# Decode attention over 64 heads: K and V loaded from two queues, PV moved in front of the next pair's score matmuls, both output weights loaded last

## The chip, the core and the metric

The kernel runs on one core of a Trainium2 chip. The metric is the device time of one execution in microseconds; shown before the change are three runs, with a median of 674.88 us (674.65 to 674.92). Smaller is better. Names of engines: PE is TensorE, DVE is VectorE, ACT is ScalarE, POOL is GpSimd, SP is SyncE. SP and ACT can both issue DMA transfers, each into a queue of its own.

## What is computed

Two independent attention blocks, A and B, each with one query token, 32 heads, 8192 cached keys and values and a head size of 128, all bf16. The outputs of the two are joined.

```python
B, Sq, D = 1, 1, 512
H, Sk, Dh = 32, 8192, 128
q = (x @ wq).reshape(B, Sq, H, Dh)          # by head
scores = einsum("bhqd,bhkd->bhqk", q, k_cache) * Dh ** -0.5
p = softmax(scores)
o = einsum("bhqk,bhkd->bhqd", p, v_cache)
y = o.reshape(B, Sq, H * Dh) @ wo            # 4096 x 512
```

B has as many key heads as query heads, so both blocks are the same in shape. K and V of one head are 2 MB each; wq and wo of a block are 4 MB each.

## The kernel before, in words

The 64 heads are worked on in 32 pairs (`NP`), 16 of A and then 16 of B. A pair's two heads lie on the two halves of the 128 partitions: each partition holds 128 rows (`T`) of one head, 32 KB. So one `load_k(n)` and one `load_v(n)` are one transfer of 4096 KB each. K has two buffers in SBUF (`kn`), V two (`vn`).

A small recorder (`_Plan`) takes the operations in program order, one list for each engine, with the semaphore waits between them; each engine then runs its own list strictly in order. On PE the lists of pairs 3 to 28 are a loop of two pairs a round (`L0, L1 = 3, 29`); all else is straight code.

For pair n the steps are:

- `plan_mul` (DVE, line 292): K is multiplied in place by the query, in four quarters.
- `plan_red` (PE, line 301): 32 matmuls against an identity, in two halves of 16, sum the products over eighths of the head size into PSUM. The end of the second half, `red_done[n]`, frees the K buffer for `load_k(n + 2)`.
- `plan_sr` (DVE, line 310): the rest of the sum gives the scores. `plan_max`, `plan_gmax` and the first part of `plan_exp` (lines 316, 322, 325, 335, 339) find each head's maximum and hand it to all partitions.
- `plan_exp` (ACT, line 346): exp, with its row sums.
- `plan_sum` (PE and DVE, lines 351 and 354): the total of the row sums and its reciprocal.
- `plan_pv` (PE, line 367): 128 matmuls with a V tile as weights and two columns of probabilities. Its end, `pv_done[n]`, frees the V buffer for `load_v(n + 2)`.
- `plan_o` (DVE, line 377): the result, divided by the sum.

The order is a software pipeline written out by hand. In step n of the main loop PE runs: sum of pair n-1, score matmuls of pair n (both halves), first half of PV of pair n-1, the maximum's transpose of pair n, second half of PV of pair n-1, the maximum's broadcast of pair n.

All large loads are issued by SP, in this order: wq of A, K0, wq of B (into the second V buffer), then in step n K(n+1), waiting for `red_done[n-1]`, and V(n), waiting for `pv_done[n-2]`. Wo of A follows V12, into the buffer `wbuf` that held wq of A. At step 29 PE does the wo matmuls of A (`plan_relayout`, `plan_wo`, `plan_y`, lines 402 to 426); then the first half of wo of B (heads 0 to 15) is loaded into the same buffer, and the rest of it in four groups (8, 4, 2, 2 heads, `WOG`) behind V31. V31 is loaded in two halves. The wo matmuls of B's first half stand at the end of step 31, those of the rest after PV of pair 31. `plan_out` transposes the result and stores it.

ACT's own queue has only the two loads of x, 1 KB each.

Of the kernel before, what the change touches and what calls it, by code (L numbers as in the profile page):

```python
# [11 lines left out]
P = 128  # L12
# [11 lines left out]
class _Plan:  # L24
# [6 lines left out]
    def wait(self, eng, mark):  # L31
        if mark is None:
            return
        ctr, val = mark
        if val <= 0 or self.waited.get((eng, ctr.name), 0) >= val:
            return
        self.waited[(eng, ctr.name)] = val
        self.prog[eng].append((None, ctr, val))

    def op(self, eng, fn, ctr=None, needs=(), inc=1):  # L40

        for m in needs:
            self.wait(eng, m)
        self.prog[eng].append((fn, ctr, inc))
        if ctr is None:
            return None
        ctr.n += inc
        return ctr, ctr.n
# [46 lines left out]
def bass_concat_heads__mha_block_cached__gqa_block_cached__decode_kernel(  # L95
# [18 lines left out]
    NA = 2  # L114
    H, Sk, Dh = ks[0].shape[1:]
    D = xs[0].shape[2]
    NOUT = wos[0].shape[1]
# [19 lines left out]
    with ExitStack() as st:  # L137
# [8 lines left out]
        wbuf = sb("wbuf", [P, C * H * Dh], BF16)  # L146
        wq_buf = [wbuf[:], vn[:, 1].rearrange("p t d -> p (t d)")]
        wq_sb = [b.rearrange("p (c n) -> p c n", c=C) for b in wq_buf]
        wo_sb = wbuf[:].rearrange("p (j n) -> p j n", n=NOUT)
        qbc = sb("qbc", [P, NP, Dh], BF16)  # L150
        pt = sb("pt", [P, 2, T, 2], BF16)
        s_sb = sb("s_sb", [P, 2, T], F32)
# [34 lines left out]
        def ctr(name):  # L187
            return _Ctr(nc, st, name)

        s_x = ctr("s_x")  # L190
        s_w = [ctr("s_w%d" % a) for a in range(NA)]
        s_wo = [ctr("s_wo%d" % i) for i in range(5)]
        s_v2 = ctr("s_v2")
        s_k = [ctr("s_k%d" % i) for i in range(NK)]
        s_v = [ctr("s_v%d" % i) for i in range(NV)]
        s_out = ctr("s_out")
# [3 lines left out]
        def dma(eng, dst, src, c, needs=()):  # L200
            return op(eng, lambda e: e.dma_start(dst, src), c, needs, inc=16)  # L201
# [27 lines left out]
            k_in[n] = dma("SP", kn[:, n % NK].rearrange("p t d -> p (t d)"), src, s_k[n % NK],  # L229
                          [red_done.get(n - NK)])  # L230

        def load_v(n, parts=1):
            a, i = divmod(n, PA)
            src = vs[a][0, 2 * i:2 * i + 2].rearrange("h (p t) d -> (h p) (t d)", p=HP)
            dst = vn[:, n % NV].rearrange("p t d -> p (t d)")
            w = T * Dh // parts
            v_in[n] = [dma("SP", dst[:, i * w:(i + 1) * w], src[:, i * w:(i + 1) * w],
                           s_v2 if i else s_v[n % NV],
                           [q_done[1] if n == 1 else pv_done.get(n - NV)])
                       for i in range(parts)]  # L240

        def load_wq(a):
            wq_in[a] = dma("SP", wq_buf[a], wqs[a].rearrange("(p c) n -> p (c n)", p=P), s_w[a])
# [1 line left out]
        def load_wo(a, g):  # L245
            h0, n = WOG[a][g]
            src = wos[a][h0 * Dh:(h0 + n) * Dh, :].rearrange("(p j) n -> p (j n)", p=P)
            wo_in[a, g] = dma("SP", wo_sb[:, h0:h0 + n, :].rearrange("p j n -> p (j n)"), src, s_wo[g],
                              [q_done[0] if a == 0 else wo_done[0]])


        for a in range(NA):
# [37 lines left out]
        def plan_mul(n, c):  # L290
            k = kn[:, n % NK, c * CT:(c + 1) * CT, :]
            mul_done[n, c] = op("DVE", lambda e: e.tensor_tensor(  # L292
                k, k, qbc[:, n:n + 1, :].broadcast_to([P, CT, Dh]), ALU.mult),
                c_mul, [k_in[n], qbc_ready[n]])
# [14 lines left out]
        def plan_sr(n, h):  # L309
            sr_done[n, h] = op("DVE", lambda e: e.tensor_reduce(  # L310
                s_sb[:, n % 2, h * HT:(h + 1) * HT],
                rps[:, h, :].rearrange("p (t d) -> p t d", d=DW), AX.X, ALU.add),
                c_sr, [red_done[n], p_done.get(n - 2)])
# [36 lines left out]
        def plan_sum(n):  # L350
            m = op("PE", lambda e: e.matmul(misc[:, 0:2], ones_f[:], rsum[:, n % 2, :],  # L351
                                            start=True, stop=True), c_pe,
                   [p_done[n], misc_free[0]])
            r_done[n] = misc_free[0] = op("DVE", lambda e: e.reciprocal(  # L354
                rinv[:, n, :], misc[:, 0:2]), c_dve, [m])

        def plan_pv(n, t0, t1):
            parts = v_in[n]
            for i in range(t0 * len(parts) // T, (t1 * len(parts) - 1) // T + 1):
                wait("PE", parts[i])  # L360
            wait("PE", p_done[n])
            wait("PE", o_done.get(n - 2))

            def mm(e):
                r = None
                for t in range(t0, t1):
                    r = e.matmul(acc[:, n % 2, 0:2], vn[:, n % NV, t, :], pt[:, n % 2, t, :],  # L367
                                 start=(t == 0), stop=(t == T - 1))
                return r
            if t1 == T:  # L370
                pv_done[n] = op("PE", mm, c_pv)
            else:
                op("PE", mm)

        def plan_o(n):
            a, i = divmod(n, PA)
            o_done[n] = op("DVE", lambda e: e.tensor_tensor(  # L377
                oD[:, a, 2 * i:2 * i + 2], acc[:, n % 2, 0:2], rinv[:, n, :], ALU.mult),
                c_dve, [pv_done[n], r_done[n]])
# [16 lines left out]
        def plan_relayout(a, g):  # L396
            h0, n = WOG[a][g]
            z = z_n[0] % 2
            z_n[0] += 1
            s = P // n  # L400
            zv = zb[:, z, :].rearrange("p (h s) -> p h s", s=s)
            m = op("DVE", lambda e: e.tensor_tensor(  # L402
                zv, oD[:, a, h0:h0 + n].unsqueeze(2).broadcast_to([P, n, s]),
                mask[n][:, None, :].broadcast_to([P, n, s]), ALU.mult),
                c_dve, [sel_ready[n], o_done[a * PA + (h0 + n) // 2 - 1], z_free.get(z)])
            z_free[z] = op("PE", lambda e: e.matmul(misc[:, 0:n], zb[:, z, :], jsel[n][:],  # L406
                                                    start=True, stop=True), c_pe, [m, misc_free[0]])
            o2_ready[a, g] = misc_free[0] = op("DVE", lambda e: e.tensor_copy(
                o2[:, a, h0:h0 + n], misc[:, 0:n]), c_dve, [z_free[z]])

        def plan_wo(a, g):

            h0, n = WOG[a][g]

            def mm(e):
                r = None
                for j in range(h0, h0 + n):
                    for i in range(NQ):
                        r = e.matmul(qyp[:, i:i + 1], wo_sb[:, j, i * P:(i + 1) * P],  # L419
                                     o2[:, a, j:j + 1], start=(j == 0 and i == 0),  # L420
                                     stop=(j == H - 1 and i == NQ - 1), skip_group_check=True)
                return r
            wo_done[a] = op("PE", mm, c_pe, [o2_ready[a, g], wo_in[a, g], qy_free[0]])

        def plan_y(a):
            qy_free[0] = op("DVE", lambda e: e.tensor_copy(yT[:, a, :], qyp[:, 0:NQ]), c_dve,  # L426
                            [wo_done[a]])
# [7 lines left out]
            wait("SP", done)  # L435


        L0, L1 = 3, 29
        marks = {}

        load_wq(0)
# [5 lines left out]
        for n in range(NP + 1):  # L447
            marks[n] = len(pl.prog["PE"])
            last = n == NP
            if n == L1:  # L450
                plan_relayout(0, 0)
                plan_wo(0, 0)
                plan_y(0)
            if n + 1 < NP:
                load_k(n + 1)
            if n == 1:
                for j in range(4):
                    plan_q(1, j)
            if not last:
                load_v(n, 2 if n == NP - 1 else 1)  # L460
            if n == 12:
                load_wo(0, 0)
            if n == L1:
                load_wo(1, 0)
            if n == NP - 1:
                for g in range(1, len(WOG[1])):
                    load_wo(1, g)
            if not last:
                plan_mul(n, 0)
                plan_mul(n, 1)  # L470
            if n > 0:
                plan_sum(n - 1)
            if not last:
                plan_red(n, 0)
                plan_mul(n, 2)
                plan_mul(n, 3)
                plan_sr(n, 0)
                plan_red(n, 1)
            if n > 0:
                plan_pv(n - 1, 0, HT)  # L480
            if not last:
                plan_sr(n, 1)
                plan_max(n)
                plan_gmax(n)
            if n > 0:
                plan_pv(n - 1, HT, T)
            if not last:
                plan_exp(n)
            if n > 0:
                plan_o(n - 1)  # L490
            for g, (h0, k) in enumerate(WOG[1]):
                if n == max(L1 + 1, PA + (h0 + k) // 2):
                    plan_relayout(1, g)
            if n == NP - 1:
                plan_wo(1, 0)
        for g in range(1, len(WOG[1])):
            plan_wo(1, g)
        plan_y(1)
        plan_out()
# [40 lines left out]
```

## Time and profile before

| | |
|---|---|
| median of three runs | 674.88 us |
| the profiled execution, its own time | 674.97 us |
| its span, first to last instruction | 673.2 us |
| bytes read | 285.21 MB, 424 GB/s over the span |
| PE, DVE, ACT busy | 70%, 53%, 7% |
| mean granted clock of PE | 0.738 |
| score matmuls (line 301), 1024 | 293.2 us busy |
| multiplies (line 292), 128 | 286.8 us busy |
| PV (line 367), 4096 matmuls | 113.0 us busy |
| an issue of a large transfer on SP | 0.33 us |
| K, issue to landing, median | 25.5 us in A, 25.3 in B |
| V, issue to landing, median | 31.6 us in A, 31.4 in B |

The profile is of one execution. Its times are counted from the start of the span; "idle before" is how long an engine stood before an instruction, and what ended that. The chain of waits is followed back from the last instruction, at each step to what released it. In tables by stretch, each engine has its busy time and number of instructions, and then come the granted clock of PE as a share of full speed, the mean busy share of the 16 DMA engines, and the GB/s that they moved. DMA queue q1 is SP's and q10 is ACT's.

### The profile page before, as it was taken

The page shows a single profiled execution, that of the slowest core. Times are in us where ns is not written, and L with a number is a line of the kernel's source. Part 1 is how long each engine was busy: PE and PEld are TensorE (multiplying, and loading weights), DVE is VectorE, ACT ScalarE, POOL GpSimd, SP SyncE. Part 2 cuts the span into 40 slices and gives each one's busy share as a digit, 9 for nine tenths or more (in the row PEclk, how much of TensorE's full clock was granted, in tenths as well). Part 3 has the DMA queues.
Part 4 walks back from the last instruction along what each step waited for, and adds up shares of the span by engine and source line. Part 5 has one row for each costly group of instructions (what it writes and reads, how often), then busy time and mean ns, then how long its engine had stood idle before and what let it go on. Part 6 is the DMA issues. An engine that isn't in the chain of part 4 may idle for free.

```text
span 673.2 us, 12408 instructions
## 1 busy us (share of the span) xinstructions
PE 468.9 (70%) x5712; PEld 275.8 (41%) x5712; DVE 359.4 (53%) x345; ACT 43.9 (7%) x171; POOL 2.1 (0%) x13
## 2 busy tenths in 40 slices
PE   2575887566778776665667787676677776778857
PEld 1233444244444343442344444344444433455526
DVE  1554556565555665615655556566555565645451
ACT  1120000000000000000000000000000000000000
POOL 1000000000000000000000000000000000000000
PEclk9787877667788766776677887666778765677866
DMA  9999999999999999999999999999999999999994
GB/s 374 436 435 431 429 423 432 427 434 436 433 430 432 430 428 432 434 434 430 431 432 428 432 432 436 428 432 434 428 430 432 436 427 434 432 429 429 427 424 202
DMA packets 10550, 285.48 MB, mean 424 GB/s; under 512 B 1186, under 2 KB 1188, under 8 KB 1572
## 3 DMA queue, kind: packets, MB, share of 16 engines
q1 hardware_dynamic: 10528, 285.22, 98.7%
q8 instruction: 13, 0.21, 0.1%
q14 instruction: 5, 0.04, 0.0%
q10 hardware_dynamic: 4, 0.00, 0.0%
HBM read 285.21 MB, written 0.00 MB: 424 GB/s over the span
## 4 chain that ended last, share of the span: by engine, by line
DMA 61%; PE 26%; DVE 8%; issue 5%; SPq 0%
DMA kn<-in_A_k_cache_dram 31%; DMA kn<-in_B_k_cache_dram 30%; PE rps L301 23%; DVE kn L292 7%; PE acc L367 2%; PE qyp L419 1%; PE mtp L322 0%; PE bmp L430 0%; DVE zb L402 0%; PE bmp L335 0%; PE misc L406 0%; PE misc L351 0%; SPq L201 0%; DVE oD L377 0%; DVE yT L426 0%
## 5 line engine op out<-in xcount | busy, mean ns | idle before, releaser
L301 PE MATMUL rps<-kn,ident 128*128 128x512 bf16 x1024 | 293.2, 457 | 144.0 <-DVE kn L292 144.0
L292 DVE TENSOR_TENSOR kn<-kn,qbc 128x4096 bf16<-128x4096 bf16 x128 | 286.8, 2283 | 90.9 <-DMA kn<-in_A_k_cache_dram 63.3
L301 PEld LDWEIGHTS rps<-kn,ident 128*128 128x128 bf16 x1024 | 114.2, 114 | 310.4 <-DVE kn L292 140.5
L367 PEld LDWEIGHTS acc<-pt,vn 128*128 128x128 bf16 x4096 | 110.6, 97 | 14.8 <-issue 7.5
L310 DVE TENSOR_REDUCE s_sb<-rps 128x64 f32<-128x512 f32 x64 | 44.3, 691 | 132.2 <-PE rps L301 132.2
L367 PE MATMUL acc<-pt,vn 128*128 128x2 bf16 x4096 | 113.0, 164 | 0.5 <-issue 0.5
L339 ACT ACTIVATE negb<-bmp 128x1 f32<-128x1 f32 x32 | 5.5, 171 | 594.4 <-PE bmp L335 594.4
L351 PE MATMUL misc<-rsum,ones_f 128*128 128x2 f32 x64 | 18.2, 354 | 36.7 <-ACT pt L346 36.4
L351 PEld LDWEIGHTS misc<-rsum,ones_f 128*128 128x128 f32 x64 | 15.5, 301 | 39.6 <-ACT pt L346 38.8
L377 DVE TENSOR_TENSOR oD<-acc,rinv 128x2 bf16<-128x2 f32 x32 | 5.1, 159 | 48.3 <-PE acc L367 48.3
L346 ACT ACTIVATE pt<-s_sb,negb 64x128 bf16<-64x128 f32 x64 | 27.9, 435 | 1.8
L335 PE MATMUL bmp<-gm,hrow 1*128 1x1 f32 x128 | 23.6, 285 | 0.5 <-DVE gm L325 0.5
L325 DVE TENSOR_REDUCE gm<-mtp 1x2 f32<-1x128 f32 x32 | 8.9, 279 | 27.8 <-PE mtp L322 27.8
L335 PEld LDWEIGHTS bmp<-gm,hrow 1*128 1x128 f32 x128 | 21.0, 230 | 1.3 <-issue 0.7
L322 PE MATMUL mtp<-ident_f,m 128*1 128x128 f32 x64 | 12.1, 271 | 1.1 <-DVE m L316 1.1
L346 ACT ACTIVATION_READ_ACCUMULATOR pt<-s_sb,negb 64x1 f32 x64 | 11.7, 182 | 0.0
L274 PE MATMUL qyp<-wbuf,xb 128*64 128x512 bf16 x32 | 5.6, 484 | 6.2 <-DMA wbuf<-in_A_wq_dram 4.1
L316 DVE TENSOR_REDUCE m<-s_sb 128x1 f32<-128x128 f32 x32 | 9.2, 286 | 1.1
L419 PE MATMUL qyp<-o,wbuf 128*128 128x1 bf16 x256 | 7.3, 165 | 1.1 <-issue 0.9
L419 PEld LDWEIGHTS qyp<-o,wbuf 128*128 128x128 bf16 x256 | 7.0, 102 | 1.3 <-issue 0.9
L274 PE MATMUL qyp<-vn,xb 128*64 128x512 bf16 x32 | 5.5, 477 | 2.3 <-ACT qbc L282 2.3
L354 DVE RECIPROCAL rinv<-misc 128x2 f32<-128x2 f32 x32 | 5.3, 164 | 2.9 <-PE misc L351 2.9
(34 smaller groups left out, 27.1 us busy)
## 6 DMA issues: line engine op xcount, KB each, us to landing
kn<-in_A_k_cache_dram SPq DMA_DIRECT2D x16, 4096.0 KB, 25.5
vn<-in_A_v_cache_dram SPq DMA_DIRECT2D x16, 4096.0 KB, 31.6
kn<-in_B_k_cache_dram SPq DMA_DIRECT2D x16, 4096.0 KB, 25.3
vn<-in_B_v_cache_dram SPq DMA_DIRECT2D x15, 4096.0 KB, 31.4
wbuf<-in_A_wq_dram SPq DMA_DIRECT2D x1, 4096.0 KB, 12.4
vn<-in_B_wq_dram SPq DMA_DIRECT2D x1, 4096.0 KB, 30.9
wbuf<-in_A_wo_dram SPq DMA_DIRECT2D x1, 4096.0 KB, 41.2
vn<-in_B_v_cache_dram SPq DMA_DIRECT2D x2, 2048.0 KB, 23.0
```

What stands on the lines that cost most here:

```text
L274: r = e.matmul(qyp[hh * HP:(hh + 1) * HP, :].rearrange("p (i d) -> p i d", d=Dh), xb[:, a, c, hh * HP:(hh + 1) * HP], w, start=(c == 0), s ...
L292: mul_done[n, c] = op("DVE", lambda e: e.tensor_tensor(k, k, qbc[:, n:n + 1, :].broadcast_to([P, CT, Dh]), ALU.mult), c_mul, [k_in[n], qbc ...
L301: r = e.matmul(rps[:, h, :].rearrange("p (t d) -> p t d", d=DW), ident[:], kn[:, n % NK, h * HT:(h + 1) * HT, i * DW:(i + 1) * DW], start= ...
L310: sr_done[n, h] = op("DVE", lambda e: e.tensor_reduce(s_sb[:, n % 2, h * HT:(h + 1) * HT], rps[:, h, :].rearrange("p (t d) -> p t d", d=DW ...
L316: m_done[n] = op("DVE", lambda e: e.tensor_reduce(m1[:, n % 2:n % 2 + 1], s_sb[:, n % 2, :], AX.X, ALU.max), c_dve, [sr_done[n, 1]])
L322: m = op("PE", lambda e: e.matmul(mtp[0:1, 0:P], m1[:, n % 2:n % 2 + 1], ident_f[:], start=True, stop=True), c_pe, [m_done[n], i_identf, g ...
L325: gm_done[n] = op("DVE", lambda e: e.tensor_reduce(gm[:, n % 2, :], mtp[0:1, 0:P].rearrange("o (h p) -> o h p", h=2), AX.X, ALU.max), c_dv ...
L335: r = e.matmul(bmp[:, 0:1], hrow[0:1, h, :], gm[0:1, n % 2, h:h + 1], start=(h == 0), stop=(h == 1))
L346: p_done[n] = op("ACT", lambda e, h=h, q=q: e.activation(pt[q, n % 2, :, h], s_sb[q, n % 2, :], AF.Exp, bias=negb[q, n:n + 1], scale=scale ...
L351: m = op("PE", lambda e: e.matmul(misc[:, 0:2], ones_f[:], rsum[:, n % 2, :], start=True, stop=True), c_pe, [p_done[n], misc_free[0]])
L367: r = e.matmul(acc[:, n % 2, 0:2], vn[:, n % NV, t, :], pt[:, n % 2, t, :], start=(t == 0), stop=(t == T - 1))
L419: r = e.matmul(qyp[:, i:i + 1], wo_sb[:, j, i * P:(i + 1) * P], o2[:, a, j:j + 1], start=(j == 0 and i == 0), stop=(j == H - 1 and i == NQ ...
```

## The change

Three things are changed.

1. V is loaded by ACT's queue, K and the weights by SP's. V31 is one transfer again. V0 waits for K0 to land; V1 waits for the projections of B, as before; each later V(n) waits for PV of pair n-2, as before. In ACT's list the issue of V(n) stands behind exp of pair n-1 and in front of exp of pair n.
2. PV of a pair is one block of 128 matmuls, and stands right behind the sum of its pair, in front of the next pair's score matmuls. `plan_o` stands in DVE's list behind the multiplies of the next pair.
3. Wo of A and wo of B are loaded behind K31 on SP's queue. B's goes to the first K buffer and so waits for the score matmuls of pair 30. All wo matmuls come last, behind PV of pair 31; the relayouts that need no later pair come in step 31 in front of it. PE's loop now covers pairs 3 to 30.

```diff
-        wo_sb = wbuf[:].rearrange("p (j n) -> p j n", n=NOUT)
+        wo_sb = [b.rearrange("p (j n) -> p j n", n=NOUT)
+                 for b in (wbuf[:], kn[:, 0].rearrange("p t d -> p (t d)"))]
...
-        def load_v(n, parts=1):
+        def load_v(n):
             a, i = divmod(n, PA)
             src = vs[a][0, 2 * i:2 * i + 2].rearrange("h (p t) d -> (h p) (t d)", p=HP)
             dst = vn[:, n % NV].rearrange("p t d -> p (t d)")
-            w = T * Dh // parts
-            v_in[n] = [dma("SP", dst[:, i * w:(i + 1) * w], src[:, i * w:(i + 1) * w],
-                           s_v2 if i else s_v[n % NV],
-                           [q_done[1] if n == 1 else pv_done.get(n - NV)])
-                       for i in range(parts)]
+            need = {0: k_in[0], 1: q_done.get(1)}.get(n, pv_done.get(n - NV))
+            v_in[n] = dma("ACT", dst, src, s_v[n % NV], [need])
...
-            wo_in[a, g] = dma("SP", wo_sb[:, h0:h0 + n, :].rearrange("p j n -> p (j n)"), src, s_wo[g],
-                              [q_done[0] if a == 0 else wo_done[0]])
+            wo_in[a, g] = dma("SP", wo_sb[a][:, h0:h0 + n, :].rearrange("p j n -> p (j n)"), src, s_wo[a][g],
+                              [q_done[0] if a == 0 else red_done[NP - 2]])
...
-        def plan_pv(n, t0, t1):
-            parts = v_in[n]
-            for i in range(t0 * len(parts) // T, (t1 * len(parts) - 1) // T + 1):
-                wait("PE", parts[i])
-            wait("PE", p_done[n])
-            wait("PE", o_done.get(n - 2))
+        def plan_pv(n):
 
             def mm(e):
                 r = None
-                for t in range(t0, t1):
+                for t in range(T):
                     r = e.matmul(acc[:, n % 2, 0:2], vn[:, n % NV, t, :], pt[:, n % 2, t, :],
                                  start=(t == 0), stop=(t == T - 1))
                 return r
-            if t1 == T:
-                pv_done[n] = op("PE", mm, c_pv)
-            else:
-                op("PE", mm)
+            pv_done[n] = op("PE", mm, c_pv, [v_in[n], p_done[n], o_done.get(n - 2)])
...
-        L0, L1 = 3, 29
+        L0, L1 = 3, 31
...
             if n == L1:
-                plan_relayout(0, 0)
-                plan_wo(0, 0)
-                plan_y(0)
+                for a, g in ((0, 0), (1, 0), (1, 1), (1, 2)):
+                    plan_relayout(a, g)
...
             if not last:
-                load_v(n, 2 if n == NP - 1 else 1)
-            if n == 12:
+                load_v(n)
+            if n == NP - 1:
                 load_wo(0, 0)
-            if n == L1:
-                load_wo(1, 0)
-            if n == NP - 1:
-                for g in range(1, len(WOG[1])):
+                for g in range(len(WOG[1])):
                     load_wo(1, g)
             if not last:
                 plan_mul(n, 0)
                 plan_mul(n, 1)
             if n > 0:
                 plan_sum(n - 1)
+                plan_pv(n - 1)
             if not last:
                 plan_red(n, 0)
                 plan_mul(n, 2)
                 plan_mul(n, 3)
+            if n > 0:
+                plan_o(n - 1)
+                if n >= L1:
+                    plan_relayout(1, n - L1 + 3)
+            if not last:
                 plan_sr(n, 0)
                 plan_red(n, 1)
-            if n > 0:
-                plan_pv(n - 1, 0, HT)
-            if not last:
                 plan_sr(n, 1)
                 plan_max(n)
                 plan_gmax(n)
-            if n > 0:
-                plan_pv(n - 1, HT, T)
-            if not last:
                 plan_exp(n)
-            if n > 0:
-                plan_o(n - 1)
-            for g, (h0, k) in enumerate(WOG[1]):
-                if n == max(L1 + 1, PA + (h0 + k) // 2):
-                    plan_relayout(1, g)
-            if n == NP - 1:
-                plan_wo(1, 0)
-        for g in range(1, len(WOG[1])):
+        plan_wo(0, 0)
+        plan_y(0)
+        for g in range(len(WOG[1])):
             plan_wo(1, g)
         plan_y(1)
         plan_out()
```

More of the change, by code (lines that the diff above doesn't have):

```diff
@@ L191, in bass_concat_heads__mha_block_cached__gqa_block_cached__decode_kernel @@
         s_w = [ctr("s_w%d" % a) for a in range(NA)]
-        s_wo = [ctr("s_wo%d" % i) for i in range(5)]
-        s_v2 = ctr("s_v2")
+        s_wo = [[ctr("s_wo%d_%d" % (a, g)) for g in range(len(WOG[a]))] for a in range(NA)]
         s_k = [ctr("s_k%d" % i) for i in range(NK)]
@@ L418, in mm @@
                     for i in range(NQ):
-                        r = e.matmul(qyp[:, i:i + 1], wo_sb[:, j, i * P:(i + 1) * P],
+                        r = e.matmul(qyp[:, i:i + 1], wo_sb[a][:, j, i * P:(i + 1) * P],
                                      o2[:, a, j:j + 1], start=(j == 0 and i == 0),
```

## The prediction

> **What bounds the kernel now.** I read the slices of the page first, then busy time in stretches of the span, the chain of waits, and the instructions in order of time at both ends and in one pair of the middle.
>
> ```profile
> span 673.2 us, 12408 instructions
> ...
> PE 468.9 (70%) x5712; PEld 275.8 (41%) x5712; DVE 359.4 (53%) x345; ACT 43.9 (7%) x171; POOL 2.1 (0%) x13
> ...
> q1 hardware_dynamic: 10528, 285.22, 98.7%
> ...
> q10 hardware_dynamic: 4, 0.00, 0.0%
> ```
>
> ```profile
> 200.00:300.00 100.00, 70.54 (x840) 41.53 (x840) 54.70 (x50) 5.76 (x25) 0.00 (x0) 0.72 1.01 433
> ...
> 660.00:664.00 4.00, 3.10 (x85) 2.94 (x83) 0.64 (x4) 1.15 (x5) 0.00 (x0) 0.77 0.93 373
> 664.00:668.00 4.00, 3.51 (x126) 3.34 (x123) 0.14 (x1) 0.00 (x0) 0.00 (x0) 0.50 0.27 102
> ```
>
> The last two columns are the DMA engines' busy share and GB/s. From 17 us to about 663 us that share is 0.98 or more in every long stretch; no compute engine is above 70%. So DMA bounds all but both ends, and what matters is how many bytes there are, at what rate, and what is left to do after the last ones. In steps of half a microsecond the traffic falls from 406 GB/s at 662.5 to 94 at 666.0 and is 0 after 666.5.
>
> The rate: the chain of waits has K landings at 345.15 and 539.47 with 20 transfers of 4096 KB between (ten K, ten V), so 194.32 / 20 = 9.72 us each, and 19.4 us per pair of heads. A transfer is 128 rows of 32 KB, eight to each of 16 engines: 9.72 / 8 = 1.215 us per row.
>
> ```profile
> 642.54 0.02 issue
> ...
> 647.12 9.44 PE rps L301 x32
> ...
> 662.36 0.85 issue
> ...
> 663.94 3.20 PE acc L367 x120
> 667.14 0.46 issue
> ...
> 667.98 0.02 issue
> ...
> 668.74 1.72 PE qyp L419 x64
> 670.46 0.02 issue
> ```
>
> The end of the chain: after K31 lands at 642.54 come multiplies and score matmuls (14.0 us, to 656.56), exp, PV of pair 31, its relayout, wo matmuls and the output, to 673.2. DMA stops 6.7 us before the end. Of the two "issue" pieces, 0.85 and 0.46 us, nothing in the profile says what PE waited for.
>
> **The bytes and the rate: no change.** All 73 loads remain or (the split V31) become one; 285.2 MB stay. K and V just come from two queues. Thirty-two issues of 0.33 us leave SP for ACT; SP has nothing behind them but other transfers, and ACT is busy 7%. I take 0 for it. The trace shows no two queues with large transfers, so I bound the rate by rows: over its own stretches of 100 us it ranges from 430 to 433 GB/s, 0.7%, or 4.6 us of 660 either way. I take the middle, 0, as the row time of 1.215 us looks like that of the engine, not of the queue.
>
> The Trainium skill speaks against this part. In "DMA: Bandwidth & Descriptors", section "Issuing engines are not separate DMA queues", it says that transfers from several engines run on the same 16 DMA engines and that only issue time is saved. By it the sum is also 0 here, and the split alone can't be a gain.
>
> **Waits added to the queues.** On ACT, V0 waits for K0 and V1 for the projections of B; behind them stand only exp 0 and exp 1, which need K0 and K1 anyway, so 0. On SP wo of A, moved past the issues of K13 to K31, lets each of these go out one transfer (9.72 us) sooner in its queue; DMA is full on both sides of it, 0. Wo of B waits for the score matmuls of pair 30, whose buffer it takes; behind it on SP is only the output.
>
> **How the two queues share.** One place shows it: the two 1 KB loads of x from ACT's queue beside wq's stream from SP's.
>
> ```profile
> 1.35 0.21 ACTq L201 DMA_DIRECT2D xrow<-in_B_x_dram  x1
> ...
> 8.23 0.61 PE L256 MATMUL misc<-ones_bf,xrow 1*128 1x128 bf16 x4 [8.23 <-DMA xrow<-in_B_x_dram]
> ```
>
> Traffic begins at 3.5 us (0 GB/s from 3.0 to 3.5, 459 after). Queue q10 moved four packets (two loads, two completions), and these took until 8.23: 4.7 us, near four rows of 1.215. So I take it that the queues take turns, one row each, and that K and V each get half the rate while both have work: 19.4 us a transfer.
>
> The same page of the skill, section "Queues, rings and completion order", says that an engine drains a whole packet of some 9 to 17 descriptors from one ring before it turns to the next. That would make turns of a whole transfer; the estimate by it is K and V in alternation at full rate, with V31 up to half a transfer (4.9 us) earlier, which is my first rival. The measured 4.7 us for four turns decides for single rows.
>
> **Where V31 lands.** This is the step that sets the end. ACT's stream is in order: the issue of V(n) stands behind the exp of pair n-1. V(n)'s buffer was free long before (PV of n-2 now precedes the score matmuls of n-1), but the issue can't use that. So ACT's ring seldom holds more than one transfer and a bit.
> Count transfers from 22.95 us, where K0 lands and V0 is issued. ACT's ring has 32 (V0 to V31); SP's has 34 (wq of B, K1 to K31, and two wo). At equal shares, SP has two left, 19.4 us, when V31 lands. But for each 9.72 us in which ACT's ring is dry, SP moves one more. It is dry once: V1 needs the buffer of B's wq. That lands at 22.95 + 19.4 = 42.4 with V0; its projections took 38.63 to 46.44, 7.8 us, so V1 is issued at 50.2 and its bytes start 2.7 us later (0.80 to 3.5 at the start), 10.5 us after V0's. DMA as a whole stays busy, since K1 and K2 are queued. With DMA's end where it was, V31 lands at 666.5 - 19.4 + 10.5 = 657.6.
>
> **In the middle PE hides.** With PV in front, a pair is a chain on PE: score matmuls 8.5 to 10.0 us (the x32 rows of the chain), max and exp to the end of the accumulators 36.21 to 39.95 = 3.7 (pair 0, where no PV stood between), sum 0.6, PV 3.4: 16.2 to 17.7, below the 19.4 of DMA. The multiplies, 4 x 2.28 on DVE, run beside max's successors and PV once K has landed. Cover: 1.7 us a pair; where it is gone, the excess counts 30 times. PV's place does not warm the clock for the score matmuls: 120 of PV took 3.20 us in a stretch where the granted clock was 0.50, and it stayed there.
>
> **The tail.** Removed from the middle: wo of A (3.56 us on PE at 597.04, 0.2 of y), under full DMA, worth 0; its load at 255.28 likewise, 4 MB are 4 MB anywhere. The second half of PV between max and the broadcast (1.7 us) goes, also under DMA. Added behind V31, by rows: PV 3.4 (3.20 + 0.39 less its start), o, relayout and copy 0.76 (667.98 to 668.74), wo of A 3.56 and its y 0.2, wo of B 3.56, y to the end 2.8 (670.46 to 673.2): 14.3. Relayouts of the other groups lie before. For the unexplained stalls I bound 0 to 1.3, both of those rows, and take 0.6, as there are as many straight-line matmuls behind V31 as there were around the two. 657.6 + 14.3 + 0.6 = 672.5.
> Other floors: wo's last group at 666.5 + 0.25 (eight matmuls) + 2.8 = 669.6. V30 lands 19.4 before V31, at 638.2; PV 3.4, score matmuls 9.4, exp 3.7 give 654.7, below 657.6, so exp isn't the bound.
>
> The profiled execution took 674.97, its span 673.2, so 1.8 lies around it (the median is 674.88). The forecast is 672.5 + 1.8 = 674.3, 0.6 less than before: the 3.8 us of wo put behind V31 are nearly all that is gained by PV 31 starting 6 us earlier.
>
> **The rivals.**
> *V31 lands early; DMA's end decides.* If ACT's ring gets the larger share, V31 lands before 655; then 669.6 to 671.5, a time of 671.4 to 673.3. For: the weight of turns rests on 4.7 us of tiny loads. Against: just that. 14%.
> *V starves on ACT (slower).* Place: the issue of V(n) behind exp(n-1), one transfer deep. If SP's ring, two or three deep, gets more than half, or each issue leaves ACT's ring dry for its 2.7 us, V31 slides towards DMA's end: 666.5 + 14.3 + 0.6 = 681.4, a time of 683 at the far end. It decides from V31 at 658.3 (673.2 less 14.9): each us behind it is one us of time. For: DMA needs only one ring non-empty to stay busy, so nothing corrects V's lateness. Against: a late V holds PE, thus K's buffers, and then SP's ring runs dry and V gets it all. 20%.
> *The rate changes.* The bound above, 0.7%, is 4.6 us: 679 or 670. A row that took 1% longer, more than any stretch here shows, would cost 6.6: 681. Slower 10%, faster 5%.
> *PE becomes the bound.* If the score matmuls ran cold throughout (0.427 us at clock 0.50, 32 of them 13.7), the pair is 21.4 and 30 pairs lose 60 us. Against: they warm up after some 4 us today, out of a similar idle. 3%.
> That the change doesn't do what it says can't be: each queue's order is its engine's program order, and that has the moved loads in it.
>
> **How the numbers follow.** A measurement of this kernel tells 0.2% (1.35 us) from no change. My forecast has 48%, with V31 at 656 to 659.5, times of 673 to 676: 13 of it faster, 32 same, 3 slower. Then faster 13 + 14 + 5 = 32%, same 32%, slower 3 + 20 + 10 + 3 = 36%. Likeliest's own range: 673 to 676. The range for 8 in 10 reaches DMA's end below, 671.3, and most of V's starvation and of a slower rate above, 681.
>
> **What would show it.** Two queues with some 134 MB on ACT's and 151 on SP's; DMA share 1.00 and 430 to 433 GB/s in the middle; V's time to landing near 22 us (19.4 and the 2.7 of the start); PE waiting for V before PV in most pairs; V31 landing near 657.6 and wo matmuls of A after 662; DMA silent from 666.5. I am wrong if the rate moves by more than 0.7%, if V31 is more than 3 us off, or if PE's chain has no wait for DMA left.

## The result, and the profile after

The changed kernel is slower: 679.21 us (median of four runs, 679.13 to 679.84) against 674.9 us before (four runs); the ratio is 1.0067, with a 95% interval of 1.0055 to 1.008. The profiled execution took 679.84 us, its span 678.1, which is 4.9 longer than before's.

Line numbers are those of each run's own kernel: in the changed one the multiplies are L289, the score matmuls L298, exp L343, PV L359 and the wo matmuls L408; L201 issues every transfer. PEld is PE's loading of weights.

First the page of the changed kernel: span, engines, traffic in 40 slices of 16.95 us, and its two DMA queues.

```profile
span 678.1 us, 12388 instructions
...
PE 470.8 (69%) x5712; PEld 267.5 (39%) x5712; DVE 356.8 (53%) x345; ACT 43.9 (6%) x171; POOL 2.1 (0%) x13
...
GB/s 371 433 432 432 343 433 431 400 431 433 432 431 433 431 433 431 431 431 432 433 431 433 433 431 433 429 433 431 431 433 433 432 433 431 433 432 429 427 423 190
...
q1 hardware_dynamic: 5776, 151.00, 52.1%
q10 hardware_dynamic: 4612, 134.22, 46.0%
```

The queues have the bytes that they should have, and the engines work as long as before. Two slices stand out: the fifth (67.8 to 84.8 us) with 343 GB/s and the eighth (118.7 to 135.6) with 400. Against 432 they lack (432 - 343) / 432 x 16.95 = 3.5 us and 1.3 us of full traffic. That is 4.8 us of traffic, about the difference of the spans. Outside of them the rate is close to what it was. The same stretch of both kernels, before and then after (busy time of PE, PEld, DVE, ACT, POOL, then PE's clock, the DMA share and GB/s):

```profile
100.00:600.00 500.00, 355.24 (x4327) 210.29 (x4325) 277.34 (x253) 29.95 (x130) 0.00 (x0) 0.73 1.00 431
```

```profile
66.00:70.00 4.00, 4.00 (x14) 1.56 (x13) 1.95 (x3) 0.00 (x0) 0.00 (x0) 0.68 0.95 410
70.00:74.00 4.00, 2.90 (x15) 1.10 (x13) 0.98 (x2) 0.00 (x0) 0.00 (x0) 1.00 0.47 131
...
100.00:600.00 500.00, 361.49 (x4309) 204.74 (x4306) 277.85 (x256) 29.80 (x130) 0.00 (x0) 0.73 1.00 431
```

From 70 to 74 us the DMA engines move 131 GB/s, and from 72 to 73 nothing. Why, the instructions in order of time show, before and then after:

```profile
42.38 4.49 DVE L292 TENSOR_TENSOR kn<-kn,qbc 128x4096 bf16<-128x4096 bf16 x2 [4.40 <-DMA kn<-in_A_k_cache_dram]
...
55.07 0.33 SPq L201 DMA_DIRECT2D kn<-in_A_k_cache_dram  x1
58.69 0.33 SPq L201 DMA_DIRECT2D vn<-in_A_v_cache_dram  x1
```

```profile
45.28 0.36 ACTq L201 DMA_DIRECT2D vn<-in_A_v_cache_dram  x1
47.31 3.52 PE L359 MATMUL acc<-pt,vn 128*128 128x2 bf16 x128 [1.78 <-DMA vn<-in_A_v_cache_dram]
58.22 4.49 DVE L289 TENSOR_TENSOR kn<-kn,qbc 128x4096 bf16<-128x4096 bf16 x2 [20.22 <-DMA kn<-in_A_k_cache_dram]
...
72.72 0.33 SPq L201 DMA_DIRECT2D kn<-in_A_k_cache_dram  x1
...
75.38 0.44 ACT L343 ACTIVATE pt<-s_sb,negb 64x128 bf16<-64x128 f32 x1
75.39 0.33 ACTq L201 DMA_DIRECT2D vn<-in_A_v_cache_dram  x1
```

Before, K1 landed by 42.38, K3 was issued at 55.07 and V2 at 58.69. Now K1 lands at 58.22, for V0 and V1 share the rate with it. V1 is issued at 45.28. PV of pair 0 ends at 50.8 and V0's buffer is free. But the next V is issued at 75.39, because in ACT's list it stands behind exp 1, and exp 1 has to wait for K1, its multiplies and its score matmuls. K3 waits for the same score matmuls, until 72.72. By 70 us K2 and V1 are all but through (33 GB/s from 70 to 72), and neither queue has anything else. For 25 us a buffer was free with nothing asked for it.

The tail, from the chain of waits:

```profile
639.06 22.72 DMA vn<-in_B_v_cache_dram
...
661.83 3.59 PE acc L359 x128
...
666.43 1.58 issue
668.01 3.32 PE qyp L408 x118
...
671.66 3.64 PE qyp L408 x128
```

V31 lands at 661.78; traffic stops by 670.5, 4.0 us later than before; from there to the end it is 7.6 us in place of 6.7. These two make up the 4.9. From V31's landing to the end it is 16.3 us, of which 1.58 are a stall of PE in the wo matmuls of A.

### The profile page after: what moved, and what is told of

The parts are those of the page before. It is cut to its first block, busy times and chain, and to the rows that moved or that the text cites. A ratio compares the mean times of both kernels' runs of the same rounds, so it can differ in the third digit from the quotient of the medians.

```text
span 678.1 us, 12388 instructions
## 1 busy us (share of the span) xinstructions
PE 470.8 (69%) x5712; PEld 267.5 (39%) x5712; DVE 356.8 (53%) x345; ACT 43.9 (6%) x171; POOL 2.1 (0%) x13
## 4 chain that ended last, share of the span: by engine, by line
DMA 55%; PE 35%; DVE 5%; another core or an unknown queue 3%; issue 1%; ACT 1%; SPq 0%
DMA vn<-in_B_v_cache_dram 28%; DMA vn<-in_A_v_cache_dram 24%; PE rps L298 23%; PE acc L359 8%; DMA kn<-in_A_k_cache_dram 3%; DVE s_sb L307 2%; PE bmp L332 1%; DVE kn L289 1%; PE qyp L408 1%; PE mtp L319 1%; DVE m L313 1%; DVE gm L322 1%; ACT negb L336 0%; ACT pt L343 0%
## 5 line engine op out<-in xcount | busy, mean ns | idle before, releaser
L289 DVE TENSOR_TENSOR kn<-kn,qbc 128x4096 bf16<-128x4096 bf16 x128 | 286.7, 2283 | 104.5 <-DMA kn<-in_A_k_cache_dram 64.7
L298 PE MATMUL rps<-kn,ident 128*128 128x512 bf16 x1024 | 292.9, 457 | 16.4 <-DVE kn L289 16.4
L298 PEld LDWEIGHTS rps<-kn,ident 128*128 128x128 bf16 x1024 | 114.1, 114 | 180.8 <-issue 94.3
L359 PE MATMUL acc<-pt,vn 128*128 128x2 bf16 x4096 | 114.4, 165 | 81.8 <-DMA vn<-in_B_v_cache_dram 41.9
L359 PEld LDWEIGHTS acc<-pt,vn 128*128 128x128 bf16 x4096 | 112.1, 104 | 84.4 <-DMA vn<-in_B_v_cache_dram 43.3
L348 PE MATMUL misc<-rsum,ones_f 128*128 128x2 f32 x64 | 14.9, 302 | 39.3 <-ACT pt L343 39.0
L348 PEld LDWEIGHTS misc<-rsum,ones_f 128*128 128x128 f32 x64 | 12.2, 238 | 42.3 <-ACT pt L343 41.5
L343 ACT ACTIVATE pt<-s_sb,negb 64x128 bf16<-64x128 f32 x64 | 27.8, 435 | 1.8
L332 PE MATMUL bmp<-gm,hrow 1*128 1x1 f32 x128 | 19.3, 251 | 11.9 <-DVE gm L322 11.9
L332 PEld LDWEIGHTS bmp<-gm,hrow 1*128 1x128 f32 x128 | 16.6, 186 | 21.3 <-DVE gm L322 20.6
L319 PEld LDWEIGHTS mtp<-ident_f,m 128*1 128x1 f32 x64 | 2.7, 81 | 51.1 <-DVE m L313 51.1
L271 PE MATMUL qyp<-wbuf,xb 128*64 128x512 bf16 x32 | 7.7, 633 | 6.0 <-DMA wbuf<-in_A_wq_dram 3.9
L343 ACT ACTIVATION_READ_ACCUMULATOR pt<-s_sb,negb 64x1 f32 x64 | 11.6, 182 | 0.0
L271 PEld LDWEIGHTS qyp<-wbuf,xb 128*64 128x64 bf16 x32 | 2.4, 158 | 10.7 <-issue 6.0
## 6 DMA issues: line engine op xcount, KB each, us to landing
kn<-in_A_k_cache_dram SPq DMA_DIRECT2D x16, 4096.0 KB, 23.5
vn<-in_A_v_cache_dram ACTq DMA_DIRECT2D x16, 4096.0 KB, 23.7
kn<-in_B_k_cache_dram SPq DMA_DIRECT2D x16, 4096.0 KB, 23.7
vn<-in_B_v_cache_dram ACTq DMA_DIRECT2D x16, 4096.0 KB, 23.5
```

The lines of the kernel that those rows point to most:

```text
L271: r = e.matmul(qyp[hh * HP:(hh + 1) * HP, :].rearrange("p (i d) -> p i d", d=Dh), xb[:, a, c, hh * HP:(hh + 1) * HP], w, start=(c == 0), s ...
L289: mul_done[n, c] = op("DVE", lambda e: e.tensor_tensor(k, k, qbc[:, n:n + 1, :].broadcast_to([P, CT, Dh]), ALU.mult), c_mul, [k_in[n], qbc ...
L298: r = e.matmul(rps[:, h, :].rearrange("p (t d) -> p t d", d=DW), ident[:], kn[:, n % NK, h * HT:(h + 1) * HT, i * DW:(i + 1) * DW], start= ...
L319: m = op("PE", lambda e: e.matmul(mtp[0:1, 0:P], m1[:, n % 2:n % 2 + 1], ident_f[:], start=True, stop=True), c_pe, [m_done[n], i_identf, g ...
L332: r = e.matmul(bmp[:, 0:1], hrow[0:1, h, :], gm[0:1, n % 2, h:h + 1], start=(h == 0), stop=(h == 1))
L343: p_done[n] = op("ACT", lambda e, h=h, q=q: e.activation(pt[q, n % 2, :, h], s_sb[q, n % 2, :], AF.Exp, bias=negb[q, n:n + 1], scale=scale ...
```

## The experiments

Theory 1: DMA stands empty early on, since the issue of a V waits behind an exp on ACT's in-order list. Rival A: PV in front of the score matmuls holds PE, and through it K's buffers. Rival B: rows of two queues move slower. Every ratio below is to the kernel before, with its 95% interval.

**V on SP again**, all else as changed:

```diff
-            v_in[n] = dma("ACT", dst, src, s_v[n % NV], [need])
+            v_in[n] = dma("SP", dst, src, s_v[n % NV], [need])
```

> The changed kernel with V issued by SP again; PV in front and wo last stay. Theory 1 (the loss is DMA standing empty near 70 us and 132 us, because on ACT the issue of V2 stands behind exp 1, and one V at a time is asked for): no empty stretch, DMA ends near 666.5 us of the span, V31 lands 19.4 before that, the tail after DMA's end is the 3 to 4 us of wo's last group and the output; span 669.5 to 671.5, time 671.5 to 673.5. Rival A (PV in front of the score matmuls holds PE and so K's buffers, whatever the queue): the empty stretch stays, time 677 to 680. Rival B (rows of two queues move slower): time 674 to 675.

674.12 us, ratio 0.9986 (0.9977 to 0.9995); the profiled execution took 673.22, span 671.5. The empty stretch is gone, and this kernel is slightly faster than before, so the other two parts taken together cost nothing. Traffic ends near 667. The time is above what theory 1 allowed and inside rival B's 674 to 675, so the time alone doesn't part these two; the rate does, at 431 GB/s from 100 to 600 us with one queue and with two. PE's end is still the bound: PV 31 starts at 653.55 and there are two stalls in the wo matmuls.

```profile
70.00:74.00 4.00, 1.14 (x43) 1.15 (x43) 4.00 (x4) 0.00 (x0) 0.00 (x0) 0.55 0.95 410
```

```profile
653.55 3.38 PE acc L359 x128
...
657.95 1.28 issue
659.23 3.32 PE qyp L408 x118
...
663.26 2.13 issue
665.38 3.33 PE qyp L408 x119
```

**V on ACT, but issued in front of exp**, when PV of the pair before has freed the buffer:

```diff
-            if not last:
+            if n < 2:
                 load_v(n)
...
                 plan_pv(n - 1)
+                if n + 1 < NP and n > 0:
+                    load_v(n + 1)
```

> The changed kernel with the issue of V(n+1) moved in ACT's list to stand in front of exp n, where PV of pair n-1 has just freed the buffer; V0 and V1 stay. Theory 1: V2 goes out near 51 us in place of 75, the empty stretch near 70 us goes, DMA ends near 667, V31 lands 9 to 19 us before that; span 671 to 674, time 673 to 676. Rival A: the empty stretch stays, because K1 still lands at 58 and holds PE; time 677 to 680. Rival B: DMA ends at 671 with no empty stretch, time 677 to 680.

676.03 us, ratio 1.0019 (1.001 to 1.0029), a hair above the 673 to 676 of theory 1; profiled span 674.2. V2 is now issued within the two at 46.33 to 51.2, and both thin slices are gone:

```profile
GB/s 373 436 435 433 433 433 425 425 432 434 434 434 430 436 428 432 428 434 434 434 430 434 432 430 428 432 436 434 428 436 430 430 428 432 436 432 432 434 421 168
```

Traffic ends at 666.0 to 666.5, as before. So the place of the issue alone is worth 4 us of DMA's end. K stays on another queue and PV in front, so neither of these makes the holes: rivals A and B fall. What is left against V on SP lies, by the two chains, at the end; no run parted it further. There K31 lands near 627.7, an estimate (one transfer, 9.7 us, before V30 at 637.4); here K31 shares its rate with V and lands at 640.96, and the chain from K31 sets the end.

**The first part alone** (before's kernel, V on ACT's queue):

```diff
-            v_in[n] = [dma("SP", dst[:, i * w:(i + 1) * w], src[:, i * w:(i + 1) * w],
+            v_in[n] = [dma("ACT", dst[:, i * w:(i + 1) * w], src[:, i * w:(i + 1) * w],
...
-                           [q_done[1] if n == 1 else pv_done.get(n - NV)])
+                           [{0: k_in[0], 1: q_done.get(1)}.get(n, pv_done.get(n - NV))])
```

> The kernel before with V on ACT's queue alone; PV in two halves behind the score matmuls, wo of A in the middle. Theory 1: V2 waits for exp 1 and PV 0, later than here; empty stretch of 3 to 6 us near 70 us, and V31 shares the end with wo of B: time 678 to 684. Rival A (PV's place is the cause): no empty stretch, time 674 to 676. Rival B: no empty stretch, longer rows, 677 to 680.

689.4 us, ratio 1.0224 (1.021 to 1.0238), worse than expected and with its hole elsewhere:

```profile
279.13 43.81 DMA kn<-in_A_k_cache_dram
...
327.52 9.75 PE rps L301 x32
```

```profile
332.00:334.00 2.00, 2.00 (x8) 0.79 (x7) 0.15 (x1) 0.00 (x0) 0.00 (x0) 0.76 0.38 164
334.00:336.00 2.00, 2.00 (x11) 0.87 (x9) 0.54 (x1) 0.00 (x0) 0.00 (x0) 1.00 0.00 0
336.00:338.00 2.00, 2.00 (x42) 1.39 (x41) 0.69 (x1) 0.00 (x0) 0.00 (x0) 1.00 0.00 0
```

Wo of A, issued at 259.56, stands in SP's queue in front of a K, so this K takes 43.8 us to land in place of 25. PE has nothing to score, no buffer comes free, and the next V, behind the exp of that pair, is issued at 342.09. The split also turns order into a share: K31, behind wo of B on SP, lands at 659.0 where it landed at 642.5. That is 16.5 us later, and the chain behind it is 28.7 us in place of 30.7: the 14.5 us that the run lost. I had this hole near 70 us; the kind was right, the place wrong.

**The second part alone** (before's kernel, PV as a block in front):

```diff
                 plan_sum(n - 1)
+                plan_pv(n - 1, 0, HT)
+                plan_pv(n - 1, HT, T)
...
-            if n > 0:
-                plan_pv(n - 1, 0, HT)
...
-            if n > 0:
-                plan_pv(n - 1, HT, T)
```

> The kernel before with PV as a block in front of the next pair's score matmuls, nothing else. Theory 1: no empty stretch in the middle, DMA ends at 666.5; but at the end V30 lands at 652, one transfer behind K31, and PV 30 now holds the score matmuls of pair 31: 652 + 3.4 + 9.4 + 4.4 + 3.4 + 5.2 = 678, time 678 to 680. Rival A: an empty stretch near 70 us as well, time 682 or more. If PV's place is free at the end too, 675.

679.34 us, ratio 1.0064 (1.005 to 1.0077), as expected: no hole, traffic ends where it did, and the loss is at the end. (`plan_o` moves with PV, as in the change.)

```profile
652.38 3.57 PE acc L367 x128
655.95 8.45 PE rps L301 x32
```

V30 lands at 652.3, and the score matmuls of pair 31 wait for PV 30 behind it; before, they were over by 656.56.

**The third part alone** (both wo last; PV in two halves behind the score matmuls, V on SP; shown against the run with V on SP):

```diff
                 plan_sum(n - 1)
-                plan_pv(n - 1)
...
+            if n > 0:
+                plan_pv(n - 1, 0, HT)
...
+            if n > 0:
+                plan_pv(n - 1, HT, T)
```

> The kernel before with the third part alone: both wo loaded behind V31 on SP's one queue, all wo matmuls last; PV in two halves behind the score matmuls. Theory 1: the first two parts bring nothing and the third is the only gain. K31 lands 38.9 us before DMA's end (near 628), PV 31 starts when V31 lands near 647 and ends by 651, wo of A by 661, so only DMA's end (666.6) plus wo's last group and the output, 3 to 3.5 us, are left: span 669.7 to 671, time 671.5 to 672.8, a little below the 674.1 of V on SP with PV in front. If PV in front is a gain of its own, 674.5 or more.

671.94 us, ratio 0.9956 (0.9943 to 0.9969): the best of all, faster than both kernels. Its chain ends in DMA, as it should:

```profile
629.28 37.67 DMA kn<-in_B_wo_dram
...
667.00 0.39 PE qyp L413 x8
...
667.63 0.61 PE bmp L424 x2
```

Only the eight matmuls of wo's last group and the output stand behind the last byte. PV 31 started at 649.37 and the wo matmuls of A at 657.10, where they waited for their load.

**V0 alone on SP** (the changed kernel):

```diff
-            need = {0: k_in[0], 1: q_done.get(1)}.get(n, pv_done.get(n - NV))
-            v_in[n] = dma("ACT", dst, src, s_v[n % NV], [need])
+            need = {0: None, 1: q_done.get(1)}.get(n, pv_done.get(n - NV))
+            v_in[n] = dma("SP" if n == 0 else "ACT", dst, src, s_v[n % NV], [need])
```

> The changed kernel with V0 alone moved to SP's queue, behind K1; all other V stay on ACT, each behind the exp of the pair before. Theory 1 in two halves: the empty stretch near 70 us takes K1 landing late (58 in place of 42, since V0 and V1 share its rate) and V2's issue behind exp 1. With K1 at 42 exp 1 ends near 60, V2 goes out there, and DMA has K2 and V1 to move: no empty stretch, DMA ends near 667, V31 lands some 9.5 before; span 672.5 to 674.5, time 674.3 to 676.3. If the issue behind exp is enough by itself at any pair, there are empty stretches still, 678 or more.

679.1 us, ratio 1.0063 (1.0051 to 1.0075), above what was expected and no better than the changed kernel. K1 did land at 43.8, but PV 0, now in front of the score matmuls of pair 1, waited for V0 until 55.8, and V2 went out at 71.66. The first hole shrinks (328 GB/s from 70 to 74 us) but doesn't close, and the fifth, seventh and eighth slices are 409, 401 and 401 GB/s. So K1's late landing makes the first hole deep, but exp 1 is late without it, because PV in front lets a late V hold it too. The run isn't a clean test: from 116.70, across the seventh and eighth slices, PE stood still for 4.46 us that no semaphore explains.

```profile
43.80 4.49 DVE L289 TENSOR_TENSOR kn<-kn,qbc 128x4096 bf16<-128x4096 bf16 x2 [6.02 <-DMA kn<-in_A_k_cache_dram]
...
55.82 3.57 PE L359 MATMUL acc<-pt,vn 128*128 128x2 bf16 x128 [7.99 <-DMA vn<-in_A_v_cache_dram]
...
71.66 0.36 ACTq L201 DMA_DIRECT2D vn<-in_A_v_cache_dram  x1
```

**PV in front, wo of A back in the middle** (V on SP):

```diff
-            if n == NP - 1:
+            if n == 12:
                 load_wo(0, 0)
+            if n == NP - 1:
...
-                for a, g in ((0, 0), (1, 0), (1, 1), (1, 2)):
-                    plan_relayout(a, g)
+                plan_relayout(0, 0)
+                plan_wo(0, 0)
+                plan_y(0)
```

> V on SP and PV in front, as in the run of V on SP, but wo of A loaded behind V12 and used at step 29, as before; wo of B last. K31 and V30 then land one transfer later, near 637 and 647. Theory (V30's landing holds the score matmuls of pair 31 through PV 30): 647 + 3.5 + 9 + 4.2 + 3.5 + 0.8 + 3.6 + 2.8 = 674 of the span and 0 to 2 of stalls, time 675.5 to 678. Rival (the wo matmuls of A at the end, 3.6 us and their stalls, are what limits that run): 671 to 672.5.

676.5 us, ratio 1.0023 (1.0012 to 1.0034), as the theory had it: V30 lands at 647.4, one transfer later, and drags the score matmuls of pair 31 with it. So the place of 4 MB at the end is worth 2.4 us even though it puts 3.6 us of matmuls behind PV 31.

**V2 alone issued in front of exp** (the changed kernel):

```diff
-            if not last:
+            if not last and n != 2:
                 load_v(n)
...
                 plan_pv(n - 1)
+                if n == 1:
+                    load_v(2)
```

> The changed kernel with one issue moved: V2 in front of exp 1 in ACT's list in place of behind it. Theory 1: V2 goes out near 51 us in place of 75.4, the empty stretch from 70 to 74 us goes, and with it 3.5 us; the one near 132 may stay or go, 1.2 us. Time 674.5 to 676.5. If the stretch has another cause (K1's late landing holds PE and all follows), time 678 to 680 with the hole in its place or a little later.

677.41 us, ratio 1.0036 (1.0024 to 1.0049). From 70 to 74 us the traffic is 393 GB/s in place of 131, so moving V2's issue is enough to close this hole. But the slices at 84 and 118 us fall to 403 and 407: V3 is still behind exp 2 and goes out at 91.62. Less came back than was expected: the same wait stands in later pairs, and these two slices are thin.

## Why the prediction was wrong, step by step

The forecast was 674.3 us, 0.6 less than before; it came to 679.21, 4.3 more. That is inside the 671.3 to 681 given for 8 in 10 and outside the likeliest 673 to 676, and the sign was wrong. Of the span, 678.1 in place of 672.5, 4.2 us are V31's landing (661.78 in place of 657.6) and 1.4 the tail behind it.

- **"DMA as a whole stays busy, since K1 and K2 are queued."** This step failed, and with it "DMA's end where it was": traffic stopped at 670.5 in place of 666.5. It counted what was queued at 45 us and not when the next issue could come. K2 and V1 were all but through by 70 us; the next issues were at 72.72 (K3) and 75.39 (V2). The working had the right fact, that the issue of V(n) stands behind exp of pair n-1, but did not apply it to pair 1, where K1 was 16 us later than before. It also took wq of B to land at 42.4, which kept V1's issue late on paper (50.2; it was 45.28). In the experiments the early issue brings DMA's end back by 4 us, V2 alone by 2.5 (no traffic from 668.0).
- **The rival with the right place.** The slower rival named the issue behind exp, one transfer deep, but priced it at the end of the kernel, as V31 sliding towards DMA's end. It didn't slide: V31 landed 8.7 us before the traffic stopped, 8.9 were predicted. The loss came at the start, in a time below that rival's 683.
- **The shares of the queues, and V31's place.** The shares came out: K and V take 23.5 to 23.7 us to land, in the median, with both queues at work. The reading behind them was wrong. Traffic does not begin at 3.5 us: before's slices have 657 GB/s from 1.5 to 2.0 us and 393 from 2.0 to 2.5, and 0 up to 3.5 only because a row is counted where it starts. So neither the 4.7 us for four turns nor the 2.7 us from issue to bytes stands. And the dry spell of 10.5 us at V1 did not come: V1 was issued at 45.28, before V0 had landed at 47.3. That V31 still lay 8.7 us before DMA's end is luck; where ACT's queue lost these us instead was not worked out. A slip without weight: wo of A stood behind K13 already, and moves past K14 to K31.
- **The rate.** Right: 431 GB/s from 100 to 600 us in both kernels. The Trainium skill, "DMA: Bandwidth & Descriptors", section "Issuing engines are not separate DMA queues", says that starting transfers on several engines saves only issue time, and this case agrees: the second queue brought no bandwidth. Its loss came from the order of the issues.
- **PE hides in the middle.** Right from 140 us on. Before that there was less room than 1.7 us a pair: a stall of 1.42 us in PE's list, at 119.36, lies in the second thin slice. With every V early that slice has 425 GB/s, but no such stall fell there, so that run doesn't part the two. With V2 alone early it has 407 with PV whole (3.58 us at 116.22), so the slice is thin without the stall too. What the stall adds isn't shown.
- **The tail behind V31.** 14.3 + 0.6 was predicted, 16.3 measured. The term most mis-sized is the stall: 1.58 in place of 0.6. PV (3.6) and the two wo (3.6 each, with the stall left out) are within 0.2 each.
- **The parts' values.** The first was taken at 0 and costs 5.1 us in this kernel (679.21 against 674.12) and 14.5 alone. The second, taken as hidden, costs 4.4 alone at the end, 2.2 beside wo last (674.12 against 671.94). The third is the gain, 2.9 us alone. It was priced as nearly eaten up by the 3.8 us of wo behind V31; with V on one queue V31 lands before wo of A and these matmuls wait for loads anyway.

## What to carry to other kernels

Before moving a load to a compute engine's queue, write down for each buffer when it comes free and when the engine's in-order list reaches the issue; the gap between is lost depth, and it first shows where the pipeline starts. Where DMA is at its rate all through the middle, as here at 431 GB/s with one queue or two, the order of the loads decides the end: put last those bytes that need the least work behind them, and keep the bytes with the longest chain in front in the same queue, for two queues share the rate and give the order away (K31 landed at 640.96 with two queues, near 627.7 with one).

## What the runs showed of the hardware

PE stood still where no semaphore explains it, 0.5 to 2.2 us at a time and once 4.46, in straight code and in the first round of its loop, mostly among matmuls of some 27 ns each. In the changed kernel one transfer of the instruction queue (q8, 16 KB) starts between 665 and 669, around the stall from 666.43 to 668.01:

```profile
q8 instruction: 1, 0.02, 1.7%
```

It starts between 665.4 and 665.6 and takes 1.1 us, so it is over early in the stall, 1.3 us before the stall ends. In the run with V on SP one starts between 662.8 and 663.0, takes 1.1 us too, and ends 1.4 us before the stall from 663.26 to 665.38 does. That PE waits there for its own code fits both, but no run took the fetch away, so it isn't shown.

Also, 64 matmuls of PV took 1.75 us at a granted clock of 1.00 (before, from 114.70) and 128 took 3.57 at 0.50 (changed kernel, from 661.83): here PV's time hardly depends on that clock. Nor did such a run of matmuls raise it: through the 246 wo matmuls from 668.01 to 675.30 it stayed at 0.50.
